# Moving the w1 sums of a linear-attention and MLP block from GpSimd to VectorE, and two steps of them into the sweep

## The chip, the cores and the metric

One core of a Trainium2 chip runs the whole kernel. The metric is the device time of one execution in microseconds.

## The reference, cut to what matters

```
x: 2048 tokens x 576          (S x D)
g = sigmoid((x * gate_w).sum(-1))
a = linear attention, 32 heads of 18: q, k, v = x @ wqkv; phi(t) = where(t > 0, t + 1, exp(t)) + 1e-6
    kv = phi(k)^T v, z = sum of phi(k);  o = phi(q) kv / (phi(q) z);  a = o @ wo
b = gelu(layernorm(x) @ w1 + b1) @ w2 + b2        w1: 576 x 4608, w2: 4608 x 576
out = g * a + (1 - g) * b
```

All is float32. A product is made of high and low parts: ScalarE rounds an operand to a shorter form (the high part), VectorE subtracts it from the operand (the low part), and TensorE adds high x high, high x low and low x high.

## The kernel before, in words

All operations are recorded through one helper, so every row of the profile has its line (L112), and they are told apart by the names of their tiles. Each engine, and the queue of SyncE (SP) that issues nearly all transfers, works strictly in the order of the program.

**Sweep** (to some 206 us). Sixteen tiles of 128 tokens, in three slots each; `at(n, f)` puts a job into slot n. A tile's keys and queries are projected and the sums of keys x values kept in PSUM. In between, the layer-normalised tokens y of the MLP are made, two tiles at a time: `load_pair` fetches a pair (and rows with its means and scales, through DRAM in `moments`), `normal_pair` applies them, `sum_pair` makes four differences, `split_pair` and `split_tails` make high and low parts, in four parts of two blocks, and `store_pair` writes them to `yd` in DRAM. Five of the eight pairs are done here; they are called (half, j). `load_wo` and `load_wv` fetch the weights of the value stage.

**Value stage** (to some 280 us). `project_values` makes the weight `wp`; then a loop over 16 token tiles, where `transpose_q`, `attend`, `normalize`, `weigh` (on POOL) and `attend_out` make g * a and store it in `late_acc`. `during(i, f)` puts a job behind tile i: pairs (1,1) and (1,2) are normalised on POOL here, and the data of step 0 of w1 is loaded, summed and split.

**MLP.** Both products of the MLP use a scheme with seven products in place of eight: blocks of w1 (A11, A12, A21, A22) and of y (B11 and so on) and sums of them (S1 to S4, T1 to T4). The hidden columns are cut into 18 chunks, the tokens into two halves; a **step** k is one chunk for one half, so there are 36: 18 for the first half of the tokens and 18 for the second. Two steps are a **window** of 14 slots. In each slot x, `product` does one of the seven products in the order 1, 2, 6, 5, 7, 4, 3, seven matmuls of 128x512, and `unit` twelve matmuls of 128x288 for the second matmul of the window before. Window 0 has no units. `finish_up` reads a product out of its bank: products 1, 6, 7 and 4 add up in one bank X, products 5 and 3 in Z, product 2 has its own.

The operands of w1 lie in `wa` (A11, A12, S2, S1, for products 1, 2, 6, 5) and `wb` (S3, A22, S4, for 7, 4, 3), one copy each. In the first 18 steps they are made anew: `load_w1(k)` fetches the raw blocks into `w1_raw`, `sum_w1` makes the four sums on POOL, `split_w1(k, True)` splits the first group into `wa` (ScalarE, then two operations of VectorE) and `split_w1(k, False)` the rest into `wb`, and `store_w1` keeps both in `w1d` in DRAM. The other 18 steps fetch them back block by block with `load_split_w1`, right behind the product that used the block last. A21 is loaded to the place of S3.

`do(w, x, f)` puts a job behind slot x of window w, `do_first` between the two parts of the product there. `prepare_hi`, `prepare_h_lo`, `prepare_w2_lo` make the operands of a unit two slots ahead; `sum_h` (on POOL) and `sum_w2` (on POOL) make their sums; `add_sums` adds up the results of the second matmul in `accs` at the end of a half. After the last window, `down_terms` does the last window's second matmul by the direct scheme, eight groups of 24 matmuls.

Which jobs stand where:

```
do(w, (3, 9)[odd], sum_w1, k + 1, (S1, S2))        # POOL
do(w, (4, 10)[odd], sum_w1, k + 1, (S3, S4))
do(w, (5, 11)[odd], split_w1, k + 1, True)
do(w, (6, 12)[odd], store_w1, k + 1, True)
do(w, x - 1, split_w1, k, False)                   # x = 0 or 7
```

Of the kernel before, what the change touches and what calls it, by code (L numbers as in the profile page):

```python
# [17 lines left out]
P = 128  # L18
# [17 lines left out]
PAIRS_IN_SWEEP = 5  # L36
EPS_PHI = 1e-6
# [78 lines left out]
def tile_gated_mix(ctx: ExitStack, tc: tile.TileContext, x, xm, xe, wm, we, wvm, wve, wo, um, ue, w2, b1, b2, gw, out):  # L116
# [52 lines left out]
    acc += [accrp.tile([P, D], F32, name=f"acc{i}") for i in range(TPS, NT)]  # L169
# [256 lines left out]
    def split_pair(sup, j, part, stage):  # L426
# [4 lines left out]
        act.activation(to[:, :, 0:3], src, AF.Copy)  # L431
        dve.tensor_sub(to[:, :, 3:5], src[:, :, 0:2], raw(to[:, :, 0:2]))

    def split_tails(sup, j, part):
        _, _, src, to = ys[sup, j, part]

        dve.scalar_tensor_tensor(to[:, :, 2], raw(to[:, :, 2]), low_rows[:, 0:1], src[:, :, 2], op0=OP.mult, op1=OP.add)
# [7 lines left out]


# [80 lines left out]
    load_x(ORDER[4])  # L527
    add_products(first[1], 1)
# [30 lines left out]
    at(3 * 3, load_wo)  # L559
    at(3 * 3 + 2, load_wv)  # L560
    for n, f in ((24, gates_in), (25, gates_act), (26, gates_out)):
        at(n, f, 0)
    def prepare_scale(q, n):
        at(n, scale_in, q)
        at(n + 1, scale_out, q)
        at(n + 2, share_moments, q)

    for q in range(PAIRS_IN_SWEEP):
# [10 lines left out]
        for part, n in enumerate(parts):  # L579
            at(n, split_pair, sup, j, part, lambda part=part: y_stages[part])  # L580
            at(n, split_tails, sup, j, part)
# [5 lines left out]
    prepare_scale(NP - 1, 50)  # L587
# [156 lines left out]
    raws_at[1, 1] = pair_places(kvs_all[:, :4 * P], w1_raw[:, :12 * P], w1_raw[:, 12 * P:21 * P])  # L744
    load_pair(1, 1)
# [15 lines left out]

    def wr(k):
        at_ = w1_raw[:, :21 * P] if k else upper[:, :21 * P]
        return at_.rearrange("p (m s n) -> p m s n", m=7, s=3)

    def load_w1(k):
        r = wr(k)
        main = um[k].rearrange("p (h t f n) -> p h t f n", h=2, t=2, f=CF)
        for f, a in ((0, A11), (1, A21)):
            for h in range(2):  # L770
                sp.dma_start(r[:, a + h, 0:2], main[:, h, :, f])
                sp.dma_start(r[:, a + h, 2], four_times(ue[k][:, f * P:(f + 1) * P], h))

    def sum_w1(k, only=(S1, S2, S3, S4)):
        r = wr(k)
        for to, x0, x1, op in ((S1, A21, A22, OP.add), (S2, S1, A11, OP.subtract), (S4, A12, S2, OP.subtract),
                               (S3, A11, A21, OP.subtract)):
            if to in only:
                pool.tensor_tensor(out=r[:, to], in0=r[:, x0], in1=r[:, x1], op=op)
# [23 lines left out]
    def product(k, n, p, start=True, part=range(len(FIVE))):  # L803
# [392 lines left out]
```

## Time and profile before

| | us |
|---|---|
| median of three runs | 1180.06 (1177.16 to 1180.84) |
| the profiled execution's own time | 1180.36 |
| its span, first to last instruction | 1178.4 |
| busy: PE / PEld / DVE / ACT / POOL | 1110.6 / 1000.6 / 859.3 / 568.1 / 510.9 |

PE is the matmuls of TensorE, PEld its weight loads, DVE is VectorE, ACT ScalarE, POOL GpSimd, SPq the queue of SyncE. In rows of a timeline stand start, duration, engine, operation and tiles, how many follow each other, and in brackets how long the engine idled before and what ended that. Matmuls overlap, so PE looks busy where it is only slowed; its pace is better read from marks that come back in each step. The granted clock is given as a share of full speed.

### The profile page before, as it was taken

What the parts mean: (1) busy time and instruction counts of PE and PEld (TensorE: products, weight loads), DVE (VectorE), ACT (ScalarE), POOL (GpSimd) and SP (SyncE); (2) the same over time, 40 slices, a digit from 0 to 9 for tenths busy, and PEclk for the clock granted to TensorE, in tenths of its full rate; (3) what the DMA queues carried; (4) which work ended last, traced back from release to release, by engine and by line L of the source; (5) the groups of instructions that cost most, each with busy time, mean ns of one, the idle gap of its engine ahead of it and who ended that gap; (6) DMA issues with size and microseconds to landing.
All of it is one profiled execution on the core that took longest, in us unless ns stands there. A gap on an engine that the chain in (4) does not pass through costs nothing.

```text
span 1178.4 us, 17946 instructions
## 1 busy us (share of the span) xinstructions
PE 1110.6 (94%) x6651; PEld 1000.6 (85%) x6651; DVE 859.3 (73%) x1115; ACT 568.1 (48%) x911; POOL 510.9 (43%) x352
## 2 busy tenths in 40 slices
PE   8999999998588999998999999999999999999988
PEld 8989998987477888887888878988999999999978
DVE  4568886997477878787887877787666656656684
ACT  6557664444445544454444454445444444444440
POOL 1112113872666546575554755435325325324400
PEclk9999999999889999999999999999999999999999
DMA  5557985946844444434454448847434434435422
GB/s 176 156 88 190 234 204 87 386 163 205 317 157 155 158 153 140 135 116 151 157 163 145 135 136 335 314 130 236 147 102 141 143 105 147 135 107 148 128 98 81
DMA packets 113996, 194.54 MB, mean 165 GB/s; under 512 B 12927, under 2 KB 72063, under 8 KB 109686
## 3 DMA queue, kind: packets, MB, share of 16 engines
q1 hardware_dynamic: 113346, 192.82, 52.8%
q8 instruction: 52, 0.85, 0.3%
q10 hardware_dynamic: 564, 0.59, 0.2%
q14 instruction: 34, 0.28, 0.1%
HBM read 124.29 MB, written 69.09 MB: 164 GB/s over the span
## 4 chain that ended last, share of the span: by engine, by line
PE 61%; DVE 20%; DMA 8%; issue 5%; ACT 5%; SPq 1%; POOL 0%; ACTq 0%; DVEq 0%; POOLq 0%
PE ps L112 61%; DVE wa L112 6%; DVE h L112 3%; DMA w1d<-wa 3%; DVE accs L112 3%; ACT wa L112 2%; DVE wb L112 2%; DVE w_ops L112 2%; DMA t<-in_xe 1%; SPq L112 1%; DVE den L112 1%; DMA yd<-ys 1%; DMA moments<-mr 1%; DVE u L112 1%; DVE qt L112 1%
## 5 line engine op out<-in xcount | busy, mean ns | idle before, releaser
L112 PEld LDWEIGHTS ps<-w_ops,h 128*128 128x128 f32 x2856 | 430.4, 189 | 66.6 <-DVE w_ops L112 21.8
L112 PE MATMUL ps<-w_ops,h 128*128 128x288 f32 x2856 | 461.9, 297 | 17.6 <-DVE w_ops L112 15.2
L112 POOL TENSOR_TENSOR u<-u 128x512 f32<-128x512 f32 x136 | 214.4, 1601 | 230.3 <-DVE h L112 154.0
L112 PE MATMUL ps<-y,wa 128*128 128x512 f32 x1008 | 287.0, 401 | 28.5 <-DVE wa L112 21.4
L112 DVE TENSOR_TENSOR accs<-ps,accs 128x576 f32<-128x576 f32 x210 | 158.5, 755 | 126.7 <-PE ps L112 120.9
L112 PEld LDWEIGHTS ps<-y,wa 128*128 128x128 f32 x1008 | 175.9, 191 | 56.4 <-DVE wa L112 29.5
L112 ACT ACTIVATE u<-u,b1s 128x512 f32<-128x512 f32 x108 | 78.3, 725 | 275.8 <-DVE u L112 275.8
L112 PE MATMUL ps<-y,wb 128*128 128x512 f32 x756 | 202.9, 393 | 4.5 <-ACT u L112 2.6
L112 DVE TENSOR_TENSOR h<-u,h 128x1024 fp32r<-128x1024 f32 x119 | 164.5, 1382 | 2.0 <-ACT h L112 2.0
L112 PE MATMUL ps<-y 128*128 128x288 f32 (+1 forms) x1088 | 155.8, 302 | 7.9 <-ACT y L112 2.6
L112 POOL TENSOR_TENSOR w2r<-w2r 128x576 f32<-128x576 f32 x68 | 109.3, 1607 | 121.9 <-issue 40.5
L112 PEld LDWEIGHTS ps<-y 128*128 128x128 f32 x1088 | 151.8, 193 | 11.2 <-ACT y L112 3.2
L112 PEld LDWEIGHTS ps<-y,wb 128*128 128x128 f32 x756 | 132.3, 188 | 23.9 <-ACT u L112 3.9
L112 ACT ACTIVATE h<-u 128x1024 fp32r<-128x1024 f32 x119 | 125.2, 1052 | 45.4 <-PE ps L112 45.2
L112 POOL TENSOR_TENSOR w_raw<-w_raw 128x384 f32<-128x384 f32 x72 | 96.2, 1345 | 69.2 <-DMA w_raw<-in_ue 53.6
L112 DVE TENSOR_TENSOR w_ops<-w2r,w_ops 128x576 fp32r<-128x576 f32 x119 | 114.5, 962 | 0.0
L112 ACT ACTIVATE u<-ps 128x512 f32<-128x512 f32 x108 | 64.0, 592 | 92.3 <-PE ps L112 92.0
L112 DVE TENSOR_TENSOR u<-ps,u 128x512 f32<-128x512 f32 x108 | 74.1, 687 | 46.7 <-ACT u L112 23.7
L112 DVE TENSOR_TENSOR wa<-w_raw,wa 128x1024 fp32r<-128x1024 f32 (+3 forms) x37 | 64.4, 1742 | 27.0 <-ACT wa L112 26.5
L112 ACT ACTIVATE w_ops<-w2r 128x576 fp32r<-128x576 f32 x119 | 79.7, 669 | 0.0
L112 PE MATMUL ps<-wp,qt 128*128 128x288 f32 x448 | 63.6, 298 | 2.4 <-DVE qt L112 2.4
L112 POOL TENSOR_TENSOR pks<-pks,k 128x576 f32<-128x576 f32 x15 | 21.9, 1457 | 93.9 <-DVE k L112 93.8
(128 smaller groups left out, 907.1 us busy)
## 6 DMA issues: line engine op xcount, KB each, us to landing
w1d<-wa SPq DMA_DIRECT2D x18, 1280.0 KB
wa<-w1d SPq DMA_DIRECT2D x72, 320.0 KB
w2r<-in_w SPq DMA_DIRECT2D x72, 288.0 KB
y<-yd SPq DMA_DIRECT2D x14, 1280.0 KB
w1d<-wb SPq DMA_DIRECT2D x18, 960.0 KB
wb<-w1d SPq DMA_DIRECT2D x54, 320.0 KB
yd<-ys SPq DMA_DIRECT2D x15, 640.0 KB
w_raw<-in_um SPq DMA_DIRECT2D x68, 128.0 KB
```

The lines of the kernel that those rows point to most:

```text
L112: return lambda *args, **kwargs: self.tc.keep_in_program_order(op(*args, **kwargs))
```

## The change

1. `sum_w1` goes from POOL to VectorE, one sum behind each of slots 0 to 3 of a step. So that it can start so early, the raw blocks come in two groups: A11, A12, A21, A22 (the last two in the places of S2 and S1) one step ahead, right behind the split that frees their place, and A21, A22 once more for the second group. The first split stands at slot 4 of the step, where it stood at slot 5 in even and slot 4 in odd steps.
2. Steps 0 and 1 (`EARLY`) are loaded, summed on VectorE, split (`early_part`, four parts each) and stored during the sweep, slots 9 to 18; the MLP fetches their operands from `w1d`. `load_wo` and `load_wv` move from slots 9 and 11 to 18 and 20.
3. Pair (1,1) is loaded at slot 48 of the sweep and normalised on POOL while `project_values` runs; pair (1,2) takes its former place, and pair (1,3), which was normalised in window 0, is normalised at tiles 10 to 15 of the value stage.
4. Parts of y come one to a slot; the low parts are made a tile later than the high ones. In window 0, the seven parts that are left go to slots 0 to 9.
5. In window 0, product 4 gets a bank of its own, with one more copy on ScalarE and one more add on VectorE per step. The first `sum_w2` go from POOL to VectorE, and the first operands of a unit are made two slots earlier.
6. At the end, four of the seven `add_sums` go behind the last operands, two of them into the last loop, and the operands of H12 and H22 are made in slots 12 and 13, where all three of H12, H22 and H21 stood behind the last slot.

The diff, cut to its core:

```
+EARLY = 2
+    def load_w1(k, first):
+        ...
+        for f, a in ((0, A11), (1, S2)) if first else ((1, S3),):
+            for h in range(2):
+                sp.dma_start(r[:, a + h, 0:2], main[:, h, :, f])
+                sp.dma_start(r[:, a + h, 2], four_times(ue[k][:, f * P:(f + 1) * P], h))
+    def sum_w1(k, n, by=pool):
+        r = wr(k)
+        to, x0, x1, op = ((S1, S2, S1, OP.add), (S2, S1, A11, OP.subtract), (S3, A11, S3, OP.subtract),
+                          (S4, A12, S2, OP.subtract))[n]
+        by.tensor_tensor(out=r[:, to], in0=r[:, x0], in1=r[:, x1], op=op)
+    def early_part(k, part):
+        m0, m1 = 2 * part, min(2 * part + 2, 7)
+        src, to = wr(k)[:, m0:m1], y_stages[part][:, 0:m1 - m0]
+        act.activation(to[:, :, 0:3], src, AF.Copy)
+        dve.tensor_sub(to[:, :, 3:5], src[:, :, 0:2], raw(to[:, :, 0:2]))
+        dve.tensor_sub(to[64:P, :, 2], src[64:P, :, 2], raw(to[64:P, :, 2]))
...
-    at(3 * 3, load_wo)
-    at(3 * 3 + 2, load_wv)
+    at(18, load_wo)
+    at(20, load_wv)
+    for k in range(EARLY):
+        n0 = (10, 13)[k]
+        for n in range(4):
+            at(n0 + n // 2, sum_w1, k, n, dve)
+            at(n0 + 1 + n, early_part, k, n)
+            at(n0 + 2 + n, store_early, k, n)
+    at(48, load_pair, 1, 1)
+    for n in range(4):
+        at(52 + n, normal_pair, 1, 1, n % 2, n // 2, pool)
...
-    raise_pair(1, 4, 1)
-    during(4, load_pair, 1, 2)
-    raise_pair(7, 4, 2)
+    raise_pair(1, 4, 2)
+    during(9, load_pair, 1, 3)
+    raise_pair(10, 4, 3)
+    for i, blocks_ in ((11, (S2, S1, S3, A22, S4)), (13, (A11, A12))):
+        for a in blocks_:
+            during(i, load_split_w1, 0, a)
...
+        if k < 2 and n == 7:
+            act.activation(up_place(k, H12), into[n], AF.Copy)
...
-            for x, m in ((10, T3), (11, T1), (12, T2), (13, T4)):
-                do(0, x, sum_w2, 0, m)
+            for x, m in ((11, T3), (12, T1), (13, T2), (14, T4)):
+                do(0, x, sum_w2, 0, m, dve)
...
+        if EARLY <= k + 1 < HALF_TIME:
+            for n, x1 in enumerate((0, 1, 2, 3)):
+                do(w, x + x1, sum_w1, k + 1, n, dve)
+            do(w, x + 4, split_w1, k + 1, True)
+            if k + 2 < HALF_TIME:
+                do(w, x + 4, load_w1, k + 2, True)
+            do(w, x + 5, store_w1, k + 1, True)
...
-    for x, key in ((10, H11), (14, H12), (14, H22), (14, H21)):
+    for x, key in ((10, H11), (12, H12), (13, H22), (14, H21)):
...
+    for x, n, t in ((5, 2, 1), (11, 6, 1), (13, 7, 6), (14, 6, 5), (14, 3, 6)):
+        do(w, x, add_sums, p - 1, dve, n, t)
...
-                into = {1: X, 2: Yb, 6: X, 5: Z, 7: X, 4: X, 3: Z}
+                into = {1: X, 2: Yb, 6: X, 5: Z, 7: X, 4: X if w else ps[:, 4 + x // 7], 3: Z}
...
+        if s in (1, 2):
+            add_sums(p - 1, dve, *((4, 7), (7, 5))[s - 1])
```

More of the change, by code (lines that the diff above doesn't have):

```diff
@@ L168, in tile_gated_mix @@
     acc = [accs[:, spare.shape[1] + i * D:][:, :D] for i in range(TPS)]
-    acc += [accrp.tile([P, D], F32, name=f"acc{i}") for i in range(TPS, NT)]
+    acc_right = accrp.tile([P, TPS * D], F32, name="acc_right")
+    acc += [acc_right[:, i * D:(i + 1) * D] for i in range(TPS)]
     b1s = keep.tile([P, NFT], F32, name="b1s")
@@ L527, in tile_gated_mix @@
     load_x(ORDER[4])
+    for part in (True, False):
+        load_w1(0, part)
     add_products(first[1], 1)
@@ L566, in prepare_scale @@
         at(n + 2, share_moments, q)
+    for k in range(EARLY):
[4 more added lines that the diff above has]
+            at(n0 + 2 + n, store_early, k, n)
+    for part in (True, False):
+        at(9, load_w1, 1, part)
     for q in range(PAIRS_IN_SWEEP):
@@ L580, in tile_gated_mix @@
             at(n, split_pair, sup, j, part, lambda part=part: y_stages[part])
-            at(n, split_tails, sup, j, part)
+            at(n, split_rest, sup, j, part)
             at(n + 2, store_pair, sup, j, part)
@@ L759, in attend_out @@
         sp.dma_start(late_acc[i], acc[i])
[L762 to L779, printed above, removed]
     def split_w1(k, first):
@@ L864, in tile_gated_mix @@
         attend(i)
+        for job in extra_first[i]:
+            job()
         if i + 3 < NT:
@@ L997, in finish_up @@
             dve.tensor_tensor(out=u, in0=into[5 if n == 7 else n], in1=u, op=OP.add)
+            gelu(k, key, u)
+        elif n == 4 and k < 2:
+            u = up_place(k, key)
+            dve.tensor_tensor(out=u, in0=into[n], in1=u, op=OP.add)
             gelu(k, key, u)
@@ L1114, in tile_gated_mix @@
                 X, Yb, Z = bank(), bank(), bank()
-                into = {1: X, 2: Yb, 6: X, 5: Z, 7: X, 4: X, 3: Z}
-            n = UP_ORDER[i]
-            product(k, n, into[n], n in (1, 2, 5), range(0, 4))
+                into = {1: X, 2: Yb, 6: X, 5: Z, 7: X, 4: X if w else ps[:, 4 + x // 7], 3: Z}
+            n, opens = UP_ORDER[i], (1, 2, 5) if w else (1, 2, 5, 4)
+            product(k, n, into[n], n in opens, range(0, 4))
             run_jobs(w, x, 0)
@@ L1120, in tile_gated_mix @@
                 unit(w - 1, x, 0)
-            product(k, n, into[n], n in (1, 2, 5), range(4, 7))
+            product(k, n, into[n], n in opens, range(4, 7))
             finish_up(k, n, into)
```

95 lines of the change are left out of this document (46 added, 49 removed).

## The prediction

> **What bounds the kernel now.** I read the page for the shape, then the busy time by stage (columns: stretch, its length, then for PE, PEld, DVE, ACT and POOL busy us and instructions, the granted clock, DMA share, GB/s):
>
> ```profile
> 0.00:206.00 206.00, 199.08 (x1291) 187.20 (x1292) 144.45 (x313) 122.91 (x279) 39.24 (x41) 0.99 0.70 162
> 280.40:343.06 62.66, 42.77 (x178) 32.59 (x176) 38.05 (x40) 27.62 (x38) 33.00 (x23) 0.86 0.72 253
> 343.06:746.96 403.90, 376.01 (x2131) 327.38 (x2129) 321.13 (x326) 197.79 (x260) 237.11 (x157) 0.99 0.48 165
> 817.30:1131.00 313.70, 313.70 (x1864) 284.48 (x1863) 201.07 (x239) 144.40 (x201) 121.58 (x83) 1.00 0.46 136
> 1131.00:1178.40 47.40, 39.11 (x251) 37.05 (x250) 31.90 (x37) 7.09 (x10) 0.00 (x0) 0.93 0.13 50
> ```
>
> The 94% that the page gives for PE hides the loss. From 817 PE never idles and issues 1864 matmuls in 313.7 us, 5.9 per us; from 343 to 747, where the w1 operands are made, only 2131 in 403.9 us, 5.3 per us. The loss is counted by step, from the timeline of PE: the start of a step's product 7 is a mark that comes once a step.
>
> ```profile
> 393.10 1.77 PE L112 MATMUL ps<-y,wb 128*128 128x512 f32 x7
> 404.83 0.73 PE L112 MATMUL ps<-y,wa 128*128 128x512 f32 x2 [1.51 <-DVE wa L112]
> 417.98 1.77 PE L112 MATMUL ps<-y,wb 128*128 128x512 f32 x7
> 428.84 0.73 PE L112 MATMUL ps<-y,wa 128*128 128x512 f32 x2 [0.60 <-DVE wa L112]
> 431.43 1.33 PE L112 MATMUL ps<-w_ops,h 128*128 128x288 f32 x4 [1.21 <-DVE w_ops L112]
> 444.46 1.77 PE L112 MATMUL ps<-y,wb 128*128 128x512 f32 x7
> ...
> 724.55 1.77 PE L112 MATMUL ps<-y,wb 128*128 128x512 f32 x7
> 746.96 1.77 PE L112 MATMUL ps<-y,wb 128*128 128x512 f32 x7
> ```
>
> The last two marks, with no split between them, are 22.41 us apart: PE's own pace. The two steps from 393.10 take 24.88 and 26.48. The 16 steps from 343.06 (step 2) to 746.96 (step 18) take 403.9 where 16 x 22.41 = 358.6 would do: **45.3 us** lost, each time where PE waits for VectorE's split of w1 (wa) and then for the low part of w2 queued behind it. The same loss at the head:
>
> ```profile
> 281.96 6.19 PE L112 MATMUL ps<-y,wa 128*128 128x512 f32 x26 [0.83 <-DVE wa L112]
> 289.40 1.88 PE L112 MATMUL ps<-y,wb 128*128 128x512 f32 x7 [1.25 <-ACT u L112]
> 291.97 1.88 PE L112 MATMUL ps<-y,wb 128*128 128x512 f32 x7 [0.69 <-ACT u L112]
> 295.08 1.88 PE L112 MATMUL ps<-y,wb 128*128 128x512 f32 x7 [1.24 <-DVE u L112]
> 303.39 1.22 PE L112 MATMUL ps<-y,wa 128*128 128x512 f32 x2 [6.42 <-ACT wa L112]
> 307.07 8.21 PE L112 MATMUL ps<-y,wa 128*128 128x512 f32 x26 [2.46 <-DVE wa L112]
> 324.61 0.84 PE L112 MATMUL ps<-y,wa 128*128 128x512 f32 x2 [2.60 <-DVE wa L112]
> 328.84 1.33 PE L112 MATMUL ps<-w_ops,h 128*128 128x288 f32 x4 [2.91 <-DVE w_ops L112]
> 343.06 1.77 PE L112 MATMUL ps<-y,wb 128*128 128x512 f32 x7
> ```
>
> A product alone goes at some 1.6 us (26 matmuls in 6.19, so 7 in 1.67, less overlap), and half a step with its units is 22.41/2. Fourteen products and four slots with units need 22.4 + 12.8 = 35.2 us; from 280.4 to 343.06 it takes 62.7, at a mean clock of 0.86. **27.5 us** lost. And in the tail:
>
> ```profile
> 1138.24 1.18 PE L112 MATMUL ps<-y,wb 128*128 128x512 f32 x4 [0.61 <-DVE u L112]
> 1142.23 1.86 PE L112 MATMUL ps<-y 128*128 128x288 f32 x12 [0.53 <-DVE accs L112]
> 1145.80 0.80 PE L112 MATMUL ps<-y 128*128 128x288 f32 x4 [1.71 <-ACT y L112]
> 1148.43 26.36 PE L112 MATMUL ps<-y 128*128 128x288 f32 x176 [1.83 <-DVE y L112]
> ```
>
> 0.61 + 0.53 + 1.71 + 1.83 = **4.7 us**. These three places hold 77.5 us; the sweep loses only 206.0 - 199.1 = 6.9, part of it the start.
>
> **The change, part by part.** The profiled execution took 1180.36 us (span 1178.4, 2 us around it), 0.3 over the median of 1180.06; the sum is made against it.
>
> *Sums on VectorE, steps 2 to 17.* What a sum costs on each engine, and what POOL does to VectorE's splits:
>
> ```profile
> L112 POOL TENSOR_TENSOR w_raw<-w_raw 128x384 f32<-128x384 f32 x72 | 96.2, 1345 | 69.2 <-DMA w_raw<-in_ue 53.6
> L112 DVE TENSOR_TENSOR accs<-accs 128x384 f32<-128x384 f32 x20 | 11.1, 553 | 0.3
> ...
> 279.96 1.95 DVE L112 TENSOR_TENSOR wa<-accs,wa 128x1024 fp32r<-128x1024 f32 x2 [0.29 <-ACT wa L112]
> 401.12 3.65 DVE L112 TENSOR_TENSOR wa<-w_raw,wa 128x1024 fp32r<-128x1024 f32 x2 [0.58 <-ACT wa L112]
> 424.99 3.80 DVE L112 TENSOR_TENSOR wa<-w_raw,wa 128x1024 fp32r<-128x1024 f32 x2 [1.50 <-ACT wa L112]
> 395.02 5.73 POOL L112 TENSOR_TENSOR w_raw<-w_raw 128x384 f32<-128x384 f32 x4
> 400.71 6.48 POOL L112 TENSOR_TENSOR u<-u 128x512 f32<-128x512 f32 x4
> ```
>
> POOL loses 72 sums, 96.2 us. VectorE gains 64 of them here, 64 x 0.553 = 35.4 us, 4.4 a window (two steps); it idles 403.9 - 321.1 = 82.8 us there, 10.3 a window, so there is room. In return, splits meet POOL less often: 1.95 us with POOL still, 3.65 and 3.80 with POOL running. The sums delayed POOL too: the four at 395.02 pushed its u sums onto the split at 401.12. With them gone the u sums start 5.7 us earlier. The even step's split moves one slot (3.2 us) ahead, as the odd step's stands already, so its 1.51 us wait goes; in the odd step, POOL's w1 sums no longer stretch the work before the split, so I expect the 0.60 + 1.21 to go mostly. What comes late next is the raw data, since VectorE now waits for it with everything behind it:
>
> ```profile
> 412.68 0.54 SPq L112 DMA_DIRECT2D w_raw<-in_ue  x1
> 416.16 2.11 POOL L112 TENSOR_TENSOR w_raw<-w_raw 128x384 f32<-128x384 f32 x2 [5.05 <-DMA w_raw<-in_ue]
> ```
>
> The last issue at 412.68 lets the sums go at 416.16: 3.5 us. After, eight transfers (0.5 us of SP's queue each, 4 us) follow the split of the first four blocks, then 3.5 us to land: 7.5 us from the end of the split. The split comes behind slot 4 of 0 to 6, after some 2.4 us of evictions and low parts, and takes 1.95 to 3.8: it ends 4.3 to 6.1 us after slot 4, and the data is there after 11.8 to 13.6. The first sum is due behind slot 0 of the next step, three slots or 9.6 us after slot 4. So it waits 2.2 to 4 us. Behind it stand the eviction of a unit's bank, the add of u and the low part of h, which PE needs two slots (6.4 us) on: mostly covered, by the 10.3 - 4.4 us of idle that a window has left. Four more transfers a step (A21 and A22 are fetched twice) go on a queue whose DMA share is 0.48. Bounds for the stage: all 45.3 back if cover holds everywhere; and a loss if each wait of 4 us reached PE: 16 x 4 = 64. I take half of the loss back, **-22**, since both waits that I can name (1.51 in an even step; 0.60 + 1.21 in an odd) make 1.5 x 8 + 1.8 x 8 = 26.6 and the new wait eats some.
>
> *Head: window 0.* Steps 0 and 1 have no split, no store, no sum here: the waits 0.83, 6.42 (a split that has to wait, by the chain of waits, for step 0's store of the same tile), 2.46 and the slow clock behind them go; product 4's own bank removes the 0.69, at 2 x (an add on VectorE and a copy on ACT) more. The first w2 sums go from POOL to VectorE and its first operands two slots earlier, against the 2.91. VectorE's y work stays: seven parts, at these rows,
>
> ```profile
> L112 DVE TENSOR_TENSOR ys<-accs,ys 128x512 fp32r<-128x512 f32 x15 | 10.3, 685 | 0.0
> L112 DVE SCALAR_TENSOR_TENSOR ys<-ys,low_rows,accs 128x256 fp32r<-128x256 f32 x15 | 7.2, 478 | 0.0
> ```
>
> 1.16 each, 7.5 in all (two are half parts); with eight u adds at some 0.7, four w1 sums, four w2 sums at 0.7, the first split and operands (some 5.5), 24 us of VectorE for 22.4 of PE: even. I give the window 29 us (6.6 for the turns of bank, copy and add that 1.25 and 1.24 above show, twice a step) and the four slots after it 14: step 2's mark at 280.4 + 43 = 323.4 against 343.06: **-20**. Bounds: -24 (nearly all) and -9 (step 1's seven operand loads of 0.32 MB queue behind 3.8 MB of y stores; the stage moves 253 GB/s now and would have to move some 300).
>
> *Sweep.* Eight sums (4.4 us), splits of two steps (two times 3.5 parts x (0.685 + an estimated 0.4, under the 0.478 of the low rows above) = 7.6) on VectorE, 24 loads, eight stores (4.5 MB) and wo and wv later. Here
>
> ```profile
> 40.00:60.00 20.00, 20.00 (x138) 19.25 (x137) 10.70 (x25) 11.50 (x29) 3.56 (x3) 1.00 0.73 181
> 60.00:80.00 20.00, 20.00 (x134) 19.12 (x133) 9.99 (x20) 8.36 (x20) 2.14 (x2) 1.00 0.69 109
> ```
>
> VectorE is idle half the time, and 12 us in 36 are covered. DMA is not so free: share 0.7. The 6.8 MB (loads and stores), at the 253 GB/s of the head, are 27 us of all queues, over the 0.3 x 40 = 12 free. Token loads are issued two tiles ahead (75 matmuls a tile, 134 to 138 in 20 us: 11 us a tile), so I take **+2**, bounds -2 and +12.
>
> *Value stage.* Pair (1,1) is normalised on POOL ahead of the fourth weighing, where POOL stands idle:
>
> ```profile
> 199.95 1.41 POOL L112 TENSOR_TENSOR qz<-accs,pks 128x576 f32<-128x576 f32 x1 [6.80 <-DVE den L112]
> ```
>
> Four operations take more than 6.8 us, but their load is moved up past it by SP, so POOL starts earlier; pair 3 goes to slots 10 to 15 for pair 2's old work. The parts come one to a slot: **0**, bounds -2 and +3.
>
> *Tail.* The operands of H12 and H22 are made a slot or two earlier and four adds of slots move behind them, two into VectorE's gaps of the last loop: **-4** of 4.7 (bounds -1, -6 with the clock of 0.93).
>
> Sum: -22 - 20 + 2 + 0 - 4 = -44; 1180.4 - 44 = **1136 us**.
>
> **Rivals.** *The steps gain nothing* (VectorE takes POOL's place): the wait for raw data replaces the split's. For it: VectorE is in program order and the price of 2.2 to 4 us a step is like what goes, 2.8 a step. Against: it is early in the step, with cover. 1136 + 22 = 1158.
>
> *The two engines take turns*, a split waiting for a whole POOL operation. For it: 3.65 against 1.95. Alone, a POOL sum of w1 takes 1.0 to 1.1 (2.11 for two), a u sum 1.6 at most. Each w1 sum would then hold up VectorE by 1.05 on POOL, and after by 0.553 on its own: 8 x 0.5 = 4 us a window, 32 us in eight: 1136 + 22 - 32 = 1126. The Trainium skill has such a rule (SBUF — State Buffer, section SBUF: two separate sides): a VectorE operation with two SBUF inputs and a GpSimd operation lock each other out of a shared port for a whole instruction. The stretched splits agree with it. It also speaks against the change, as each new sum is itself such an operation.
>
> *DMA starves the sweep*: the 15 us that don't fit stall PE by 12 instead of 2: 1146.
>
> *Slower*: each step's first sum stalls PE in full, because the eight loads are issued behind a split that itself became late. 16 x 4 = 64 with no gain from the waits: 1158 + 64 = 1222. It decides once a step costs 1.4 us more than today's 25.24, since the rest saves 22 (22/16). Against it: the cover of two slots.
>
> *It does not do what it says*: no step shorter, and the head bound by DMA as now: within 0.3%. Against it: the 6.42 hangs on a store that is no longer there.
>
> **How the numbers follow.** Forecast 0.48 (its own range 1122 to 1150); turns 0.18; steps gain nothing 0.16; starved sweep 0.08; slower 0.07; no change 0.03. A measurement of this kernel tells some 0.3% from nothing, 3.5 us (the three runs span 3.7). Faster: 0.48 + 0.18 + 0.16 + 0.08 = 0.90; same 0.03; slower 0.07. The range takes in all that is faster: down to 1110 (all 45.3 us of the steps back, 1113, and the tail at -6), up to 1163 (no gain in the steps, 5 us of the sweep lost).
>
> **What would show it.** Right: marks of product 7 some 23.9 us apart between step 2 and 18; the first at 323; no wait of PE over 1.5 us in the head, and a clock near 1.0; splits of wa nearer 2 than 3.7; PE at the last loop by 1144. Wrong: a wait of VectorE on w_raw's loads in each step with PE idle behind it; a PE wait on y<-t in the sweep; PE waits on wa loads from w1d in the head.

## The result, and the profile after

The changed kernel takes 1160.4 us (median of 4 runs, 1157.1 to 1160.6) against 1180.0 for the kernel before on the same chip: a ratio of 0.983, with a 95% interval of 0.981 to 0.986. It is faster, by 19.5 us or 1.7%, which is clear of the noise; the forecast was 44. Times are medians; two disturbed executions, of 2168 and 4052 us, are left out, and the kernel whose profile is of the first one (v1 below) is read by another with the same sweep. The span went from 1178.4 to 1158.6 us, 19.8 less, and this is split by stage below.

The timeline of PE, after. The rows are the marks at which one stage ends and the next begins: the sweep's last projection, the first product of the attend loop, window 0, the products 7 of steps 2, 18 and 35, and, within the tail, the last loop.

```profile
199.02 3.96 PE L113 MATMUL ps<-y 128*128 128x288 f32 x28
...
224.81 1.30 PE L113 MATMUL ps<-wp,qt 128*128 128x288 f32 x8
...
298.22 3.13 PE L113 MATMUL ps<-y,wa 128*128 128x512 f32 x13
...
341.59 0.63 PE L113 MATMUL ps<-y,wb 128*128 128x512 f32 x2
...
736.50 1.77 PE L113 MATMUL ps<-y,wb 128*128 128x512 f32 x7
...
1119.94 1.77 PE L113 MATMUL ps<-y,wb 128*128 128x512 f32 x7
...
1129.55 25.66 PE L113 MATMUL ps<-y 128*128 128x288 f32 x192
```

The same marks before are these two and, for the rest, 280.5 (window 0), 343.06, 746.96, 1131.09 and 1178.4:

```profile
186.28 3.95 PE L112 MATMUL ps<-y 128*128 128x288 f32 x28
...
209.87 2.36 PE L112 MATMUL ps<-wp,qt 128*128 128x288 f32 x16
```

| stage | before | after | difference | forecast |
|---|---|---|---|---|
| sweep, to its last projection | 186.3 | 199.0 | +12.7 | +2 |
| value weights, to the first attend | 23.6 | 25.8 | +2.2 | 0, with the next |
| attend loop, to window 0 | 70.6 | 73.4 | +2.8 | 0 |
| window 0 and four slots, to step 2's mark | 62.6 | 43.4 | -19.2 | -20 |
| steps 2 to 17 | 403.9 | 394.9 | -9.0 | -22 |
| steps 18 to 34 | 384.1 | 383.4 | -0.7 | 0 |
| tail | 47.3 | 38.7 | -8.7 | -4 |

A few of these differences hang on the one profile: see the scatter at the head of the experiments. The gain of the head came as forecast, the tail gave twice its share, the steps gave less than half, and the sweep and the value stage took back 17.7 us. The busy time by stage, after (columns as in the prediction):

```profile
60.00:80.00 20.00, 15.10 (x91) 14.18 (x90) 13.01 (x30) 10.72 (x23) 2.23 (x2) 0.91 0.98 270
100.00:120.00 20.00, 15.29 (x100) 14.11 (x98) 12.92 (x24) 8.82 (x22) 1.51 (x2) 1.00 1.01 215
...
298.22:341.59 43.37, 39.00 (x176) 30.63 (x175) 28.78 (x45) 25.05 (x37) 3.45 (x3) 0.96 0.78 276
341.59:736.50 394.91, 373.73 (x2131) 326.00 (x2129) 328.48 (x384) 196.36 (x260) 150.63 (x97) 1.00 0.52 183
```

Between 60 and 80 us PE was always busy before, with a DMA share of 0.69; now it idles a quarter of the time and the share is 0.98. In the steps POOL fell from 237.1 to 150.6 us and VectorE rose only from 321.1 to 328.5, though it took over the sums (58 of the 64 lie in this stretch, 50.5 us): its other operations became shorter. A split of `wa`, for one, took 3.64 us on average before and 2.49 after.

### The profile page after: what moved, and what is told of

Same layout as the page of the kernel before. It is cut to its first block, busy times and chain, and to the rows that moved or that the text cites. A ratio compares the mean times of both kernels' runs of the same rounds, so it can differ in the third digit from the quotient of the medians.

```text
span 1158.6 us, 18002 instructions
## 1 busy us (share of the span) xinstructions
PE 1104.6 (95%) x6651; PEld 997.1 (86%) x6651; DVE 868.8 (75%) x1201; ACT 567.9 (49%) x917; POOL 401.0 (35%) x276
## 4 chain that ended last, share of the span: by engine, by line
PE 57%; DVE 18%; DMA 12%; issue 5%; SPq 4%; ACT 3%; POOL 0%; ACTq 0%; DVEq 0%; POOLq 0%
PE ps L113 57%; SPq L113 4%; DMA w_raw<-in_ue 4%; DVE wa L113 3%; DVE h L113 3%; DVE accs L113 3%; DVE w_ops L113 3%; DMA yd<-ys 1%; DMA w_raw<-in_um 1%; DVE den L113 1%; DMA w2r<-in_w 1%; ACT wa L113 1%; DMA xn<-in_x 1%; DMA wv<-in_wve 1%; DMA late_acc<-acc_right 1%
## 5 line engine op out<-in xcount | busy, mean ns | idle before, releaser
L113 PE MATMUL ps<-w_ops,h 128*128 128x288 f32 x2856 | 462.2, 297 | 21.2 <-DVE w_ops L113 19.2
L113 PE MATMUL ps<-y,wa 128*128 128x512 f32 x1008 | 280.9, 395 | 5.7 <-DVE wa L113 2.8
L113 POOL TENSOR_TENSOR w2r<-w2r 128x576 f32<-128x576 f32 x64 | 96.5, 1508 | 228.1 <-DMA w2r<-in_w 105.9
L113 DVE TENSOR_TENSOR h<-u,h 128x1024 fp32r<-128x1024 f32 x119 | 157.0, 1319 | 2.7 <-ACT h L113 2.6
L113 PEld LDWEIGHTS ps<-y,wb 128*128 128x128 f32 x756 | 132.8, 188 | 19.2 <-DVE u L113 0.7
L113 DVE TENSOR_TENSOR w_ops<-w2r,w_ops 128x576 fp32r<-128x576 f32 x119 | 108.0, 907 | 0.0
L113 DVE TENSOR_TENSOR u<-ps,u 128x512 f32<-128x512 f32 x110 | 75.4, 686 | 37.3 <-PE ps L113 24.3
L113 DVE TENSOR_TENSOR w_raw<-w_raw 128x384 f32<-128x384 f32 x64 | 53.8, 841 | 32.0 <-DMA w_raw<-in_ue 18.0
L113 PEld LDWEIGHTS ps<-wp,qt 128*128 128x128 f32 x448 | 61.4, 192 | 2.9 <-DVE qt L113 2.9
L113 POOL TENSOR_TENSOR pks<-pks,k 128x576 f32<-128x576 f32 x15 | 21.8, 1455 | 103.4 <-DVE k L113 103.3
```

Source lines behind the costliest of these rows:

```text
L113: return lambda *args, **kwargs: self.tc.keep_in_program_order(op(*args, **kwargs))
```

## The experiments

Each kernel ran on one chip beside the kernel before, which took 1180 to 1183 us there. "The mark" of the sweep is the row at 190.12 of the changed kernel (177.37 before). In eight profiles whose sweep is that of the changed kernel it lies between 189.6 and 192.5, so a shift below some 2 us is not a finding. Other stages scatter too where nothing in them was changed: steps 2 to 17 take 394.7 to 397.1 us in nine profiles, window 0 to step 2's mark 40.9 to 43.4 in eight. In ten profiles with the value stage of the changed kernel its first part is 25.8 us in two and 24.3 in the others, and the attend loop takes 73.4 to 77.5.

### The steps: one sum in the wrong place

In the changed kernel, VectorE (first two rows) and PE (last two) in the odd step of one window:

```profile
517.24 0.92 DVE L113 TENSOR_TENSOR w_raw<-w_raw 128x384 f32<-128x384 f32 x1 [3.26 <-DMA w_raw<-in_ue]
...
523.86 1.95 DVE L113 TENSOR_TENSOR wa<-w_raw,wa 128x1024 fp32r<-128x1024 f32 x2 [1.50 <-ACT wa L113]
```

```profile
520.68 0.79 PE L113 MATMUL ps<-w_ops,h 128*128 128x288 f32 x4 [1.12 <-DVE w_ops L113]
...
528.45 0.80 PE L113 MATMUL ps<-w_ops,h 128*128 128x288 f32 x4 [1.12 <-DVE w_ops L113]
```

VectorE stands 3.26 us at the third sum, S3, for the second group of raw blocks; then it makes h and the low part of w2 (w_ops), for which PE waits.

```
-            for n, x1 in enumerate((0, 1, 2, 3)):
+            for n, x1 in enumerate((0, 1, 3, 2)):
                 do(w, x + x1, sum_w1, k + 1, n, dve)
```

> In steps 2 to 17 the sum S3 (the only one that reads the second group of raw blocks) changes place with S4: fourth instead of third, one slot (about 3.2 us) later. Theory 'raw load': VectorE, in order, stands 3.26 us at 517.2 for that load, and the two waits of PE of 1.12 us in that window are what it delayed; the idle time on the load goes, steps 2 to 18 take 377-385 us instead of 394.9, the time is 1142-1150. Rival 'VectorE is full': GpSimd's u sums stretch it (8 of its operations at 490-500 us take 1.6 times as long), and the splits come late without the wait; steps 2 to 18 stay over 390 and the time within 5 us of 1160.

Measured: 1153.3 us, ratio 0.976 (0.973 to 0.978); steps 2 to 18 in 388.0 us. VectorE's idle time on that load (18.0 us in the groups of the changed kernel) is gone, and 6.9 us with it. The raw load was a cause, but a smaller one than expected: the second wait of the window stayed (1.09 to 1.12 us), so it had been put down to the load wrongly.

### The steps: a copy behind the gelu

That wait hangs on the 1.50 us in the row of the split: ScalarE, in order, copies the blocks to `wa` only behind the gelu of product 7, which needs an add of VectorE.

```
+            do_first(w, x + 4, split_hi, k + 1, True)     # ScalarE's copy alone, ahead of finish_up
             do(w, x + 4, split_w1, k + 1, True)           # now VectorE's two operations alone
```

> Steps 2 to 17: the sum S3 last as in the run before (388.0 us for the stage, time 1153.3), and besides ScalarE's copy of the first four blocks of the next step's w1 is issued ahead of product 7's eviction instead of behind its gelu. Theory 'copy behind the gelu': in the odd step VectorE's split waits 1.51 us for that copy, the copy for the gelu and the gelu for VectorE's own add; the low parts of h and w2 stand behind the split and PE waits 1.08-1.12 us for them, once a window. The wait goes: 8 x 1.1 = 9 us, the stage takes 378-381 and the time is 1143-1146. Rival 'VectorE is full': another operation takes the place in line and the stage stays at 386-389, the time at 1151-1155.

Measured: 1146.9 us, ratio 0.971 (0.967 to 0.974); the stage 383.4 us. Half of what was expected: VectorE no longer waits for the copy, but PE still waits 0.37 to 0.39 us for w_ops there, and in the odd step the split itself is now stretched. So both theories held in part, and what was left was VectorE's own time.

### The steps: which engine adds

```
-                do(w, x + x1, sum_w1, k + 1, n, dve)
+                do(w, x + x1, sum_w1, k + 1, n)           # on GpSimd, from the changed kernel
```

> In steps 2 to 17 the four sums of w1 go back to GpSimd, at the slots and in the order of the changed kernel; all else as changed. Theory 'VectorE in order': the sums no longer hold VectorE while the raw load is under way, but GpSimd's sums again stretch VectorE's splits (3.65 and 3.80 us before the change, 1.95 with GpSimd still) and are slower (1.05 us against 0.55): steps 2 to 18 take 398-408 us instead of 394.9, the time is 1163-1174. Rival 'engine does not matter': what the steps gained comes from the new order (split a slot earlier, second group loaded apart); 390-397 and 1156-1162.

Measured: 1163.0 us, ratio 0.984 (0.981 to 0.987); the stage 398.5 us. The part of the title that is most visible, sums on VectorE, is worth 3.6 of the 9.0 us by the changed kernel's profile, and 1.4 to 3.8 by the nine with these steps; the larger part comes from the rest of what the change did to them.

```
-        do(w, x, sum_h, p, m)
+        do(w, x, sum_h, p, m, dve if m in (S1, S4) else pool)     # on the run with copy first
```

> On top of the run with the other order and the early copy (383.4 us for steps 2 to 18, time 1146.9): of the four sums of u per window S1 and S4 go from GpSimd to VectorE, in steps 2 to 33. Theory 'shared port': GpSimd's six operations in a row at 483-493 us stretch VectorE's h, w2 and split from 1.22, 0.75 and 1.95 us to 1.4-1.8, 1.85 and 3.03; four of them less give VectorE about as much as the sums cost it (4 x 0.55 to 0.69), and at the place where PE waits: 376-381 us and 1140-1145. Rival 'VectorE is full': the added 2.5 us a window come on top; 385-395 and 1148-1158.

Measured: 1138.0 us, ratio 0.964 (0.962 to 0.966); the stage 375.7 us. Then all four u sums (this run has besides the 512-byte rows of the moments, see the sweep; its stage is read by itself):

> As the first run of this call, but S3 and S2 of u go to VectorE too, so GpSimd has the w2 sums alone. Theory 'shared port': the two sums of w1 (1.64 and 0.99 us), h and the split under the rest of GpSimd's u sums fall to 0.55, 1.22 and 1.95; VectorE pays 4 x 0.6 a window: steps 2 to 18 take 369-375 us instead of 375.7, the time is 0-6 us less. Rival 'VectorE is full': the even exchange ends, 377-385 and 2-9 us more.

Measured: 1129.1 us, ratio 0.957 (0.953 to 0.962); the stage 368.0 us, of which 358.6 are PE's own pace. The rows of POOL and VectorE in the run with the copy first:

```profile
482.96 10.07 POOL L113 TENSOR_TENSOR u<-u 128x512 f32<-128x512 f32 x6 [8.40 <-DVE h L113]
```

```profile
490.02 1.85 DVE L113 TENSOR_TENSOR w_ops<-w2r,w_ops 128x576 fp32r<-128x576 f32 x1
491.79 3.03 DVE L113 TENSOR_TENSOR wa<-w_raw,wa 128x1024 fp32r<-128x1024 f32 x2
...
497.92 0.75 DVE L113 TENSOR_TENSOR w_ops<-w2r,w_ops 128x576 fp32r<-128x576 f32 x1
```

The same operation takes 1.85 us beside POOL and 0.75 after it. The groups of VectorE in the steps show it over the whole stage: the two operations of a split of `wa`, first in the changed kernel, then with all u sums on VectorE (columns: count, busy us, mean ns):

```profile
L113 DVE TENSOR_TENSOR wa<-w_raw,wa 128x1024 fp32r<-128x1024 f32 x15 | 27.0, 1803 | 10.5 <-ACT wa L113 10.5
L113 DVE TENSOR_TENSOR wa<-w_raw,wa 64x512 fp32r<-64x512 f32 x15 | 10.3, 690 | 0.5
```

```profile
L113 DVE TENSOR_TENSOR wa<-w_raw,wa 128x1024 fp32r<-128x1024 f32 x14 | 17.0, 1214 | 0.0
L113 DVE TENSOR_TENSOR wa<-w_raw,wa 64x512 fp32r<-64x512 f32 x14 | 9.7, 690 | 0.4
```

2.49 us a split against 1.90. Additions of VectorE that read one operand from PSUM show no such effect; first before the change, where POOL was busy for 237.1 us of the stage, then with all u sums on VectorE, where it was busy for 53.8:

```profile
L112 DVE TENSOR_TENSOR accs<-ps,accs 128x576 f32<-128x576 f32 x101 | 76.0, 753 | 40.3 <-PE ps L112 39.6
```

```profile
L113 DVE TENSOR_TENSOR accs<-ps,accs 128x576 f32<-128x576 f32 x101 | 76.0, 752 | 9.9 <-PE ps L113 8.2
```

The low part of h, with both operands in SBUF, went from 1455 to 1278 ns between the same two. With each sum that leaves POOL the stage gets shorter, although VectorE is the fuller engine: it is busy 328.5 us of 394.9 in the changed kernel and 339.8 of 368.0 here. In the run with the copy first it is busy just as long, 339.8 us of 383.4, without the 64 u sums: what they cost it, 42.4 us, came back in its other operations. This is the mechanism of the forecast's rival "take turns". The Trainium skill (SBUF — State Buffer, section SBUF: two separate sides) has it as an exclusive lock that one side holds for a whole instruction; the trace agrees: 0.75 us became 1.85, longer by 1.1, and one u sum there is 1.7. That PE would wait for the sums themselves, which are slower on POOL, is not the reason: in the lists of waits for these stages no engine but POOL itself stands for POOL.

### The sweep

The waits of PE in the changed kernel's sweep:

```profile
72.47 5.24 PE L113 MATMUL ps<-y 128*128 128x288 f32 x28 [4.90 <-DVE k L113]
85.57 3.97 PE L113 MATMUL ps<-y 128*128 128x288 f32 x28 [0.38 <-DVE k L113]
92.34 4.00 PE L113 MATMUL ps<-y 128*128 128x288 f32 x28 [0.81 <-DVE accs L113]
114.35 2.12 PE L113 MATMUL ps<-y 128*128 128x288 f32 x14 [3.21 <-DVE k L113]
120.18 3.99 PE L113 MATMUL ps<-y 128*128 128x288 f32 x28 [1.68 <-DVE acc_right L113]
127.14 3.99 PE L113 MATMUL ps<-y 128*128 128x288 f32 x28 [1.21 <-DVE k L113]
...
190.12 3.97 PE L113 MATMUL ps<-y 128*128 128x288 f32 x28 [0.91 <-DVE k L113]
```

13.1 us, against 2.6 before. The chain of waits of that kernel leads from the one at 72 us through ScalarE to a transfer of tokens (first row below), and from the one at 127 us to the value weights and a store of y:

```profile
56.44 10.25 DMA xn<-in_x
...
99.30 10.04 DMA wv<-in_wve
109.36 14.65 DMA yd<-ys
```

What ScalarE stood at is the copy of an early part into a stage. The profile names no releaser for it; the store of that stage's last content (`w1d<-ys`) had been issued at 56.92. The exponentials for the keys stand behind the copy:

```profile
68.30 0.84 ACT L113 ACTIVATE ys<-acc_right 128x768 fp32r<-128x768 f32 x1 [6.14 <-issue]
```

Two runs took one place each. The weights at their old slots:

```
-    at(18, load_wo)
-    at(20, load_wv)
+    at(3 * 3, load_wo)
+    at(3 * 3 + 2, load_wv)
```

> The output weights and value weights are loaded at sweep slots 9 and 11 again (as before the change), nothing else differs. Theory 'late weights': the second half of the sweep's loss comes from these two loads meeting the y pairs' loads and stores at 87 to 127 us; then the waits of PE of 2.12, 1.68 and 1.21 us after 110 us go, the last sweep mark falls from 190.1 to 184-186, and the whole is 4-6 us faster than the changed kernel (1154-1156). The wait of 4.90 us at 72 us stays. Rival 'volume': the sweep moves too many bytes whatever their order; the mark stays within 2 us of 190 and the time within 2 us of 1160.

A further stage for the early parts:

```
+    def early_stage(k, part):
+        if (k, part) == (1, 0):
+            return <10P free columns of acc_right>
+        return y_stages[part - k]
```

> The first part of step 1's early w1 goes to a stage of its own and the three behind it to the stage before, so that no early part waits for a stage whose store is still under way; same bytes. Theory 'ring': ScalarE, in order, stands 6.1 us at 62 us for the store of step 0's first part, and the keys behind it stop PE for 4.90 us at 72 us; the wait goes, the mark at 190.1 falls by 4-6 us and the time to 1154-1156. Rival 'volume': the same DMA queue holds the next thing up (loads of the tokens), the 4.90 us come back as a wait of another name, and the mark falls by less than 2 us.

Measured: 1161.9 us, mark 191.5, and 1162.5 us, mark 192.6. In the first the waits past 110 us went, but the one of 4.90 us grew to 11.10, as ScalarE now stood 12.33 us at the same copy. In the second the 4.90 went with ScalarE's wait, which shows that the stage was its cause; but 5.76 and 3.98 came at 92 and 104, behind ScalarE's next waits for stores:

```profile
90.12 0.85 ACT L113 ACTIVATE ys<-accs 128x768 fp32r<-128x768 f32 x1 [6.60 <-DMA w1d<-ys]
...
100.81 0.84 ACT L113 ACTIVATE ys<-accs 128x768 fp32r<-128x768 f32 x1 [7.56 <-DMA w1d<-ys]
```

The rival "volume" was right in both: a place freed is filled again. So the next run took half of the new traffic away:

```
-    for k in range(EARLY):
+    for k in range(1, EARLY):
         n0 = (10, 13)[k]
```

> Only step 1's w1 is made in the sweep; its loads, sums, parts and stores for step 0 are left out, and step 0 (and the step that reads the same blocks again in the second half) uses step 1's operands instead, with the same loads there. So half of the sweep's new DMA traffic and half of its new work on VectorE and ScalarE are gone. Theory 'volume': the sweep is bound by its DMA queues between 60 and 130 us (share 0.98 and 1.01 of the engines); the last sweep mark falls from 190.1 by 6 us or more (to 184 or less), the time to 1148-1155. Rival 'order': one wait at one place is the cost and the rest is covered; the mark falls by less than 3 us, or comes back whole.

Measured: 1155.6 us, ratio 0.978 (0.975 to 0.981), mark 186.5. It fell by 3.7, between the two theories, and 9.1 us over the sweep before remain with one step alone. The next three looked at the time of the queue instead of its bytes.

```
-        sp.dma_start(moments[q].rearrange("a (t n) -> n a t", n=P), mr[:, q])
+        sp.dma_start(moments[q], mr[:, q].rearrange("p a t -> p (a t)"))
...
+        row = rows.rearrange("p (n c) -> p c n", c=4)[:, 2 * k + a:2 * k + a + 1].to_broadcast([P, 6, P])
```

> Same as the changed kernel, but the moments of a pair of tiles are stored as one run of 16 bytes a partition instead of four of 4 bytes, and the normalisation reads them with a stride. Theory 'volume as DMA time': the 4-byte pieces of 2 KB hold the DMA engines for some 5 to 12 us each time (DMA share near 1 at 34-41 GB/s behind the store at 52.35), so a quarter as many pieces gives that time back: the waits of PE at 72 us shrink from 4.90 to under 2, the last sweep mark falls to 180-186, the time to 1149-1156. Rival 'bytes': only the new 4.5 MB count; mark 188-191, time within 3 us of 1160. Against both: the strided row slows the normalisations on VectorE.

Measured: 1162.1 us, mark 191.6. The queue from 30 to 200 us in the changed kernel and here (packets, MB, share of 16 engines), and VectorE's normalisations in each:

```profile
q1 hardware_dynamic: 26950, 33.83, 82.1%
```

```profile
q1 hardware_dynamic: 24390, 34.09, 64.1%
```

```profile
L113 DVE TENSOR_TENSOR accs<-accs 128x768 f32<-128x768 f32 x20 | 18.9, 956 | 2.2 <-DMA accs<-moments 1.1 <-issue 0.7
```

```profile
L113 DVE TENSOR_TENSOR accs<-accs 128x768 f32<-128x768 f32 x20 | 30.7, 1549 | 1.3 <-issue 0.9
```

The difference is 18% of 170 us, 30.6 us; put down to the seven stores of 2 KB, an estimated 4.4 us each. But what the queue gave, the strided rows seem to have taken: 11.8 us more of VectorE. Dense rows, by two small transposes on TensorE a pair:

```
+            pe.transpose(ps[:4, 1 + h, KC:], mr[r, q].rearrange("p a t -> p (a t)"), ident[r, r])
+        act.activation(mrow[:, q % 2].rearrange("c (h n) -> c h n", h=2), ps[:4, 1:3, KC:], AF.Copy)
+        sp.dma_start(moments[q].rearrange("a (t n) -> (a t) n", n=P), mrow[:, q % 2])
```

> As the changed kernel, but the moments of pairs 0 to 6 are turned on TensorE (two small transposes a pair into free columns of the sums' banks, one copy on ScalarE) and stored as four rows of 512 bytes; the normalisations read dense rows as before. So the queue is relieved as in the 16-byte run (64.1% of 170 us against 82.1%) and VectorE's normalisations stay at 956 ns instead of 1549. Theory 'DMA time': the sweep's loss hangs on the queue; the last sweep mark falls from 190.1 to 178-184 and the time to 1148-1155. Rival 'VectorE in order': the sums and parts added on VectorE hold keys and queries up by themselves; mark 187-191, time 1157-1161.

Measured: 1163.9 us, ratio 0.986 (0.984 to 0.988), mark 197.9. The queue's share is 62.2%, but TensorE, in order, now waits for VectorE ahead of the transposes: 4.88 us at 173.3 and 4.76 at 193.7. The waits that are not the transposes' own sum to 4.1 us. The following runs leave the last pairs as they were, and stand on the run with two u sums on VectorE:

> The best run so far (sum order, early copy, two u sums on VectorE: 375.7 us for steps 2 to 18, 1138.0) with the moments of pairs 0 to 4 stored as rows of 512 bytes, turned one slot later than in the run that tried it; pairs 5 and 6 keep the 4-byte store, so the two waits of TensorE of 4.88 and 4.76 us for them are not there. Theory 'DMA time': the rest of that run's sweep waited 5.5 us instead of 12.7; the last sweep mark is 181-185 instead of 190.1, the time 1129-1133. Rival 'VectorE in order': mark 187-192, time 1135-1139.

> As the run before in this call, but step 1's raw w1 and the output and value weights are loaded right behind step 0's raw w1, at some 33 us, where the queue's share is 0.25, instead of at 40, 87 and 98 us. Theory 'idle queue': the mark falls 2-4 us below that run's, the time 2-4 us. Rival 'tokens late': 3.8 MB (some 15 us) stand ahead of the tokens of tiles 5 and 6 in the queue, PE waits for y<-t ahead of 60 us, and the mark is 2 us or more above that run's.

> As the first run of this call, but the eight early sums of w1 go to GpSimd, which is busy 28 of 180 us in the sweep, two of the four of a step one slot earlier. Theory 'VectorE in order': 4.4 us of VectorE less at 50 to 75 us, and the keys and queries come earlier; mark 1-3 us below that run's. Rival 'shared port': GpSimd's 1.05 us sums stretch VectorE's parts by as much; mark within 1 us.

Measured: v1 1135.4 us, v2 1144.2, v3 1132.9. The sweep of v1 is read in the run with all u sums on VectorE: mark 186.4. Loading everything early (v2) is the worst, mark 195.0: a wait of 11.03 us at 70 us for tokens that stand behind it, as its rival said. GpSimd for the early sums (v3): mark 186.6, no difference. Last, the transposes at the end of a tile:

```
+        at(11 + 6 * q if q < PAIRS_IN_SWEEP else n + 2, share_moments, q)
```

> As the run with all u sums on VectorE (368.0 us for steps 2 to 18, 1129.7), but the moments of pairs 0 to 4 are turned at the end of a tile, behind its last product, where TensorE's next write to those banks is a tile away. Theory 'DMA time holds the sweep': what was left of the old waits there is 4.4 us and the turns' own cost 4.4 (1.55 and four of 0.70 behind ScalarE's copy); these go, the last sweep mark falls from 186.4 to 181-183, the time to 1124-1127. Rival: the copy on ScalarE holds the keys up there instead; mark 185-188, 1128-1131.

Measured: 1127.1 us, ratio 0.952 (0.950 to 0.955), the shortest of all. Mark 185.7, in its rival's band, with 6.5 us of waits:

```profile
70.26 3.99 PE L113 MATMUL ps<-y 128*128 128x288 f32 x28 [0.57 <-DVE k L113]
...
111.14 2.98 PE L113 MATMUL ps<-y 128*128 128x288 f32 x14 [2.67 <-DVE k L113]
```

The large wait at 72 us is down to 0.57. The one at 111 still hangs, by the chain of waits, on a token load of 9.70 us issued at 99 behind the weights and a pair. What is shown: the stores in 4-byte pieces, in a queue that is nearly full, hold some 4 to 6 of the 12.7 us. The early weights together with the dense rows were not tried; the rest of the sweep's loss stays open.

### The value stage

```
-        at(52 + n, normal_pair, 1, 1, n % 2, n // 2, pool)
+        during(0, normal_pair, 1, 1, n % 2, n // 2, pool)
```

> The four normalisations of pair (1,1) on GpSimd go from the value stage to behind the first attend, its sums one attend later; the small operations of the last pair's scale stay where the change put them. Theory 'GpSimd in the value stage': they stretch VectorE's own operations (1 us for tiny ones) and so hold wp, qt: from the sweep's end to the first attend it takes 33.8 us now against 28.9 to 30 before; it falls by 3-5 us, and the time by 2-5 unless the attend loop gives it back. Rival 'scale moved': the three small operations behind the projections are the cost; the stretch falls by less than 1.5 us.

Measured: 1162.4 us. From the sweep's last projection to the first attend (the expectation counts from another mark) it takes 23.5 us instead of 25.8: the waits for wp went from 1.48 and 1.03 us to 0.15 and none. But the wait for qt behind it grew from 2.66 to 4.52, and the loop took 78.7 us, 5.3 more. Against all ten profiles both differences shrink, to 0.8 us gained in most and 1.2 to 5.3 lost. Part of the loop's scatter is the clock: two profiles with an unchanged value stage and the same wait for qt (the run with the third sum later, 3.58 us, and the one with two u sums on VectorE, 3.55) differ in the granted clock (the third figure from the right) of the loop's first 10 us, 0.68 and 1.00, and take 77.2 and 73.7 us for the loop:

```profile
222.92:232.92 10.00, 6.42 (x32) 6.17 (x31) 9.19 (x16) 2.57 (x7) 9.32 (x9) 0.68 1.05 103
```

```profile
225.71:235.71 10.00, 6.45 (x50) 6.14 (x49) 9.19 (x16) 3.85 (x10) 9.33 (x9) 1.00 1.08 117
```

In the run with the normalisations later the first 10 us have a clock of 0.76. There VectorE's four small operations of the last pair's scale met POOL's normalisations (four in 7.71 us from 219.66):

```profile
221.91 0.15 DVE L113 TENSOR_TENSOR mt<-mr 128x2 f32<-128x2 f32 x1
222.09 1.75 DVE L113 TENSOR_TENSOR mt<-mt 128x2 f32<-128x2 f32 x1
223.88 1.76 DVE L113 TENSOR_SCALAR mt<-mt 128x2 f32<-128x2 f32 x1
225.67 1.72 DVE L113 TENSOR_TENSOR mr<-mr,mt 128x2 f32<-128x2 f32 x1
```

Operations on two numbers a partition take 1.72 to 1.76 us in three of the four rows, nearly the length of one of POOL's, 1.93.

```
-    for n, f in ((50, scale_in), (56, scale_out), (56, share_moments)):
+    for n, f in ((50, scale_in), (51, scale_out), (52, share_moments)):
```

> As the other run of this call, and the last pair's three small scale operations go back from behind the projections to the slot after their square root (as before the change), GpSimd's normalisations staying where they are. Theory 'scale behind the projections': these four operations (1.11, 0.93, 0.17, 0.84 us under GpSimd) stand ahead of qt, for which PE waits 2.64 us; that wait falls below 0.5 and the time by 2-3 us against the other run. Rival 'GpSimd': the parts of qt and the normalisation of queries are stretched anyway; the wait stays over 1.5 us and the time within 1 us.

Measured: 1129.3 us (1127.6 to 1130.2), against 1127.1 (1123.9 to 1127.9) of the other run. The waits for qt and wp are gone and the part to the first attend is 23.4 us, as before the change, but no time is gained: in the attend loop PE now waits for VectorE ahead of the transposes of queries (1.78, 1.04, 0.60, 2.15 us), and window 0 starts only 1.4 us earlier, 1.1 of which the sweep had already.

### The head and the tail

```
-                into = {..., 4: X if w else ps[:, 4 + x // 7], 3: Z}
+                into = {..., 4: X, 3: Z}
```

> In window 0 product 4 shares its bank with products 1, 6 and 7 again, as in all other windows: no copy on ScalarE and no add on VectorE for it. Theory 'own bank saves a turn': the wait of 0.69 us a step comes back: from window 0's start to step 2's mark 44.5-46 us instead of 43.4, time 1161-1163. Rival 'VectorE has it back': without the add (0.7 us a step) the operands behind it come earlier; 42-43.5 us, time 1158-1160.

Measured: 1161.3 us; window 0 to step 2's mark in 41.4 us. The wait of 0.69 us is there again in both steps, and the stage is still within the 40.9 to 43.4 us of the profiles with the own bank. The own bank is worth at most its two waits, and no time that these runs can tell.

```
-    for x, key in ((10, H11), (12, H12), (13, H22), (14, H21)):
+    for x, key in ((10, H11), (14, H12), (14, H22), (14, H21)):
     # and all sums of slots ahead of the last loop again
```

> The tail alone as before the change: operands of H12 and H22 made at the end of the last window, and all sums of slots ahead of the last loop. Theory 'operands late': from step 33's mark to the end it takes 38.7 us with the change and 47.3 before; the three waits ahead of the last loop (0.53, 1.71, 1.83 us) and the slower clock behind them come back, 46-47.5 us, time 1167-1169. Rival 'only the waits': they alone come back, 42-43.5 us, time 1163-1166, and the rest of the 8.65 us has another source.

Measured: 1166.2 us, ratio 0.988 (0.986 to 0.990); the tail takes 43.0 us from step 35's mark (which the expectation calls step 33's). PE there:

```profile
1131.91 1.88 PE L113 MATMUL ps<-y 128*128 128x288 f32 x12 [0.53 <-DVE accs L113]
1135.48 0.79 PE L113 MATMUL ps<-y 128*128 128x288 f32 x4 [1.69 <-ACT y L113]
1136.84 23.65 PE L113 MATMUL ps<-y 128*128 128x288 f32 x176 [0.57 <-DVE y L113]
```

It is 4.4 us longer, in the band of its rival "only the waits", and the waits of PE in it, with one of 0.61 us ahead of these rows, sum to 3.4. The last is 0.57 instead of 1.83; I put that down to the order of slot 14, where this run still has the low parts ahead of the sums (not tried alone). What remains to the 47.3 us of before, 4.3, is mostly that 1.26 and the pace of the last loop: the same 176 matmuls took 26.36 us before and take 23.65 here, 2.71 less. The granted clock fits. In the windows of before, PE runs at 0.88 and then, though never idle, at 0.77; in this run a shorter gap is followed by 1.00:

```profile
1140.00:1150.00 10.00, 5.93 (x33) 5.10 (x32) 9.96 (x11) 3.56 (x4) 0.00 (x0) 0.88 0.00 0
1150.00:1160.00 10.00, 10.00 (x61) 10.00 (x61) 5.58 (x8) 0.00 (x0) 0.00 (x0) 0.77 0.16 61
```

```profile
1129.00:1139.00 10.00, 7.21 (x48) 6.39 (x47) 9.96 (x11) 3.76 (x5) 0.00 (x0) 1.00 0.00 0
1139.00:1149.00 10.00, 10.00 (x77) 10.00 (x76) 8.00 (x11) 0.00 (x0) 0.00 (x0) 1.00 0.24 90
```

That the shorter gap is why the clock stayed at 1.00 was not tried alone.

## Why the prediction was wrong, step by step

- **Sweep, +2: wrong by 10.7.** The prediction found 27 us of new transfers for 12 us of free queue and then took 2, because tokens are issued two tiles ahead. That step failed: with the queue at a share of 0.98 a token load takes 10 us, and what the lead of two tiles doesn't cover is ScalarE, which stood 6.14 us for a stage that was still being stored, with the keys behind it. It also turned bytes into time at 253 GB/s, while its own row had a share of 0.69 at 109 GB/s; the runs with the moments show how long small pieces hold a queue. For this stage its rival "starved sweep", with 12 us, came out, at a chance of 0.08. Less than half of the loss was won back by any run, and the rest is open.
- **Steps, -22: wrong by 13.** The size of the new wait was right where it came (2.2 to 4 us forecast, 3.26 in the row above; 18.0 us over the stage), but it came at the third sum and not the first, and "mostly covered" was wrong: h and the low part of w2 stand right behind it (6.9 us with the order of sums). The second wait that was to go "mostly" was not POOL's doing but the copy's behind the gelu (4.6 us). And "splits meet POOL less often" held in the odd step (1.95 us) more than in the even: there POOL's u sums, six in a row once the w1 sums are gone, run straight over the split (3.03 us for two operations), 2.49 on average where it had been 3.64. The price of a sum was off too: 0.84 us on VectorE on average, not the 0.553 of a sum in the sweep. With all three mended the stage is 368.0 us, 35.9 better than before, near the bound of -45.3 that the prediction had.
- **Value stage, 0: wrong by 5** (4 to 8 in the ten profiles). The prediction counted POOL's idle time and not what stands behind the normalisations on VectorE. With the scale's small operations back in their old place the waits for wp and qt went, though the normalisations stayed; others came in the loop, and no run won the time back. How the 5 us divide between VectorE's operations beside POOL and the slower clock behind the wait for qt is open.
- **Head, -20: right.** 19.2 us, and up to 21.7 in other profiles; no wait over 1.25 us and a clock of 0.96. The mark of 323.4 was missed by 18.2 because everything ahead of it was 17.7 late.
- **Tail, -4: right in its mechanism, half in size.** Undoing the change to the tail costs 4.4 us, as forecast. The other 4.3, a shorter last wait and a faster clock behind it, came with the rest of the change and is argued, not tried alone; the bound of -6 had less than 2 of it.
- **Room on VectorE for the sums: right,** and more than the prediction saw: the rival "take turns" described the chip better than the forecast. It priced the w1 sums at 32 us where they gave 1.4 to 3.8; moving the u sums, which still ran beside the splits, gave 15.3 (383.4 to 368.0).
- **Luck.** The measured 1160.4 us is close to the 1158 of the rival "the steps gain nothing", but not for its reason: the steps did gain 9 us, the tail 4.7 more than forecast, and the sweep and the value stage lost 17.7.

## What to carry to other kernels

When work is moved to an engine that runs in order, write down what stands directly behind it there and when that is needed; a wait of 3 us early in a step is not covered if the next instruction in line feeds the bound engine. Price a queue by the time its transfers take in the trace, not by their bytes, and when it is full, expect a freed place to be filled by the next transfer. If VectorE and GpSimd add from SBUF side by side, VectorE's operations get longer: its idle time beside a busy GpSimd is not the whole of its room, and an operation moved off GpSimd can give VectorE back as much as it costs. Before a stage's time is compared between two kernels by one profile each, see how far it scatters in profiles where it was not changed.

## What the runs showed of the hardware

- A store of 2 KB in pieces of 4 bytes cost the queue 4.4 us more than in pieces of 16, estimated from the shares above (18% of 170 us for seven). The Trainium skill (DMA: Bandwidth & Descriptors, section Rules for kernel authors) says that a non-contiguous last dimension becomes one descriptor per element; the packets of under 512 bytes fell from 5676 to 2997 when four elements went together, and agree: seven stores of 128 pieces in place of 512 would be 2688 fewer.
- An operand of VectorE read with a step of 16 bytes, broadcast over six rows, took 1549 ns where the dense one took 956.
- Beside operations of GpSimd of 1.9 us, a VectorE operation on 128x2 elements took 1.75 us; in the kernel before, with GpSimd still, it took 0.16 to 0.17. Additions of VectorE with one operand in PSUM took 753 and 752 ns where GpSimd was busy for 237.1 and for 53.8 us of the stage.
- TensorE's granted clock stayed at 0.77 for 10 us of unbroken work behind 10 us in which PE was busy 5.93, and at 1.00 behind 10 us with 7.21. The busy time of 10 us doesn't decide it: in the first 10 us of the attend loop PE was busy 6.42 us at a clock of 0.68 in one run and 6.45 at 1.00 in another.
